# First pair's keys in three pieces, and a rewritten order of every engine's work, in a fused attention and feed-forward kernel

## The chip, the cores and the metric

The kernel runs on 1 core of one Trainium2 chip. The metric is device time in microseconds (us) of one launch; lower is better. The engines are called as in the profile: PE (TensorE products), PEld (its weight loads), DVE (VectorE), ACT (ScalarE), POOL (GpSimd) and SP (SyncE, which only issues transfers here).

Runs are compared in one state, "fast": not more than 1.5% above the fastest of the same kernel; the others are called slow. A **look** is the one run of a kernel that was profiled. Every ratio below is the mean time of one kernel's fast runs over the mean of the other's in the same rounds on the same chip, so it is not quite the ratio of the medians beside it. Beside each run stands the mean granted clock of PE as a share of full speed. As the records of the clock hold only 1.0 and 0.5, I work out a run's **halved time** as 2 x (1 - mean clock) x span. It is good to about 0.7 us, and I call a run with less than 2.5 us of it a run with a **whole clock**.

## The reference, cut to what matters

```python
def _attn_ref(q, k, v, proj):            # q, k, v: 4 x 8 heads x 768 x 64
    q_bits = (np.einsum('bhsd,dk->bhsk', q, proj) > 0)     # 6 sign bits per row
    k_bits = (np.einsum('bhsd,dk->bhsk', k, proj) > 0)
    # ... a bucket number from the bits, mask = equal buckets
    scores = np.where(mask, scale * np.matmul(q, k.transpose(0, 1, 3, 2)), -1000000000.0)
    # ... softmax, times v
def _moe_ref(x, w_in, w_out, alpha):     # x: 3072 x 512
    h = x @ w_in
    s = np.sin(alpha * h)
    g = h + s * s / (alpha + 1e-09)
    return (g @ w_out).astype(np.float32)
```

## The kernel before: the parts that matter

Heads are worked in pairs, counted from 0 (the expectations below say "second pair" for pair 1, "fifth pair" for pair 4). The 6 sign bits become 12 rows that are appended to the 64 rows of q and k, so that one product of 76 rows gives a masked score. For pair 0 VectorE writes those rows straight to their place. For every other pair it writes them to a tile `bits`, and four transfers, `row1` for pair 1, carry them over partitions to the tile `QK`:

```python
if pid == 0:
    def directf(o, e, t, h, c):          # eight bit strips of 12x384 for pair 0
        r = 32 * (2 * t + h)
        nc.vector.tensor_scalar(out=hold.slots["QK"][D:KR, t, h, HS * c:HS * c + HS], in0=two(hs, "nd")[c][r:r + NROW, 0:HS],
                                scalar1=cc[r:r + NROW, 0:1], scalar2=cc[r:r + NROW, 1:2], op0=ALU.is_gt, op1=ALU.mult)
# ... cut; for the other pairs:
    rows.append(dma(None, None, 50000, deps=[bt, hold], ..., name=f"row{pid}", get=get, dur=0.8, ...))
```

Every engine runs one written list of operations, in which the names mean: `ld30` the load of pair 3's queries, `ld31` of its keys, `tr` transposes, `ev` and `cast` copies, `hash` the products for the bits, `sc2.3` the scores and `ex2.3` the exponential of unit 2 (pair 1's first unit) block 3, `v` values, `win`/`wout` a weight's load, `fold`/`fo` its scaling, `alpha` a column of factors and `abc` its broadcast. An engine stands at an operation whose data are not there. The lists' starts, before:

```
SP    ld00 ld01 ld10 ld11 ld40 ld21 alpha ld20 ld31 ld30 row1 row1 row1 row1 row2 ...
POOL  cast1 cast1 v0 cast1 win2 win0 v3 wout0 cast1 win2 abc win1 v1 cast2 win0 wout2 ...
```

Where PE has nothing ready, the build puts warming products on the identity matrix into its list. Five buffers hold loaded tokens.

The softmax here doesn't subtract the row's maximum and nothing guards it: scores larger than these inputs give would overflow.

## Time and profile before

| | before |
|---|---|
| median of 3 runs, one of them slow | 334.84 us (334.49 to 341.64) |
| span of the profiled run, clock | 333.6 us, 0.995 |
| first score, first exponential | 14.16, 14.70 us |
| thirteenth exponential (pair 1's first) | 31.67 us |
| ScalarE changes from exp to sin | 72.14 us |
| from there to the end | 261.46 us |

### The profile page before, as it was taken

To read this page: it belongs to the slowest core of one execution; us is meant where nothing else is said; L and a number is where in the kernel's file an instruction comes from. 1 tells how busy PE (TensorE), PEld (TensorE's weight loads), DVE (VectorE), ACT (ScalarE), POOL (GpSimd) and SP (SyncE) were. 2 spreads that over 40 slices of the span, in tenths; PEclk is the share of its full clock that TensorE was granted. 3 is DMA by queue.
4 is the path that set the end of the run, shared out by engine and by line. 5 is a ranking of instruction groups with operands and counts; after the bars stand their busy time and mean duration, and the time that the engine had idled before them with its cause. 6 is when DMAs were issued, how large, how long until landed. Compare 5 with 4: busy or idle time off the path is not lost.

```text
span 333.6 us, 5767 instructions
## 1 busy us (share of the span) xinstructions
PE 322.3 (97%) x2088; PEld 157.9 (47%) x2088; DVE 221.3 (66%) x312; ACT 269.4 (81%) x387; POOL 156.0 (47%) x151
## 2 busy tenths in 40 slices
PE   8959999999999999999999999999999999999995
PEld 6533333355534444455554444455544444565542
DVE  2736853769887577987896867868837354295620
ACT  1747999999999988889989998988889898784401
POOL 1855498949766606328713664350643630012110
PEclk9989999999999999999999999999999999999999
DMA  8999797599927728344646033130201010100021
GB/s 216 195 323 347 112 174 222 83 192 204 171 36 102 158 46 119 51 85 72 115 71 142 10 52 64 36 93 2 32 6 64 1 67 0 67 29 2 24 96 68
DMA packets 92828, 32.95 MB, mean 99 GB/s; under 512 B 80112, under 2 KB 87552, under 8 KB 92672
## 3 DMA queue, kind: packets, MB, share of 16 engines
q1 hardware_dynamic: 85552, 20.00, 29.5%
q0 software_dynamic: 6800, 12.59, 15.5%
q8 instruction: 16, 0.26, 0.4%
q14 instruction: 12, 0.10, 0.1%
q10 hardware_dynamic: 448, 0.00, 0.1%
HBM read 28.32 MB, written 6.29 MB: 104 GB/s over the span
## 4 chain that ended last, share of the span: by engine, by line
PE 84%; ACT 6%; DMA 3%; DVE 3%; issue 2%; SPq 0%; POOL 0%; DVEq 0%; POOLq 0%; ACTq 0%
PE pb L796 24%; PE pp L647 20%; PE pp L748 18%; PE pp L689 10%; DMA tok<-in_q_dram 3%; PE pb L748 2%; ACT E L651 2%; PE pb L877 2%; PE pb L689 2%; PE pb L511 2%; PE pp L692 1%; DVE g L773 1%; PE pp L462 1%; PE pp L695 1%; PE pb L692 1%
## 5 line engine op out<-in xcount | busy, mean ns | idle before, releaser
L651 ACT ACTIVATE E<-pp 128x768 bf16<-128x768 f32 x192 | 148.3, 812 | 18.8 <-PE pp L647 17.4
L796 PE MATMUL pb<-wout,g 128*128 128x512 bf16 x384 | 100.9, 379 | 0.0
L647 PE MATMUL pp<-QK 76*128 76x384 bf16 x384 | 92.3, 328 | 0.8 <-DVE QK L538 0.3
L748 PE MATMUL pp<-xt,win 128*128 128x384 bf16 x432 | 74.8, 326 | 0.2
L662 POOL TENSOR_TENSOR sum<-E 128x768 bf16<-128x768 bf16 x27 | 40.3, 1494 | 62.7 <-ACT E L651 54.3
L748 PEld LDWEIGHTS <-win 128*128 128x128 bf16 x512 | 49.8, 98 | 37.3 <-issue 3.9
L569 POOL CAST QK<-F 64x768 bf16<-64x768 f32 x57 | 51.3, 905 | 26.4 <-DVE F L500 13.2
L773 DVE TENSOR_TENSOR g<-s,pp 128x768 bf16<-128x768 bf16 x54 | 50.7, 952 | 11.4 <-ACT s L764 5.7
L647 PEld LDWEIGHTS <-QK 76*128 76x128 bf16 x384 | 31.4, 97 | 54.1 <-issue 29.4
L796 PEld LDWEIGHTS <-g 128*128 128x128 bf16 x384 | 37.0, 97 | 35.1 <-issue 1.7
L755 ACT ACTIVATE s<-pp 128x768 bf16<-128x768 f32 x54 | 42.6, 804 | 13.5 <-PE pp L748 12.3
L766 POOL TENSOR_TENSOR s<-s 128x768 bf16<-128x768 bf16 x10 | 14.8, 1479 | 58.9 <-ACT s L755 33.2
L689 PE MATMUL pp<-E,V 128*64 128x385 bf16 x336 | 38.4, 333 | 0.2
L500 DVE STREAM_TRANSPOSE F<-tok 128x768 f32<-128x768 f32 x24 | 37.3, 1581 | 0.0
L717 DVE SCALAR_TENSOR_TENSOR xt<-pp,ln 128x384 bf16<-128x384 f32 x28 | 17.3, 620 | 25.9 <-ACT ln L714 25.1
L689 PEld LDWEIGHTS <-V 128*64 128x64 bf16 x384 | 20.1, 108 | 29.1 <-issue 24.1
L662 DVE TENSOR_TENSOR sum<-sum,E 128x768 bf16<-128x768 bf16 x44 | 26.5, 603 | 3.4 <-ACT E L651 1.9
L764 ACT ACTIVATE s<-s 128x768 bf16<-128x768 bf16 x33 | 27.8, 843 | 0.9
L662 DVE TENSOR_TENSOR sum<-sum 128x768 bf16<-128x768 bf16 x22 | 18.0, 818 | 11.2 <-POOL sum L662 10.0
L711 ACT ACTIVATE ln<-pp,epsb 128x384 f32<-128x384 f32 x28 | 16.3, 581 | 6.3 <-PE pp L695 4.4
L622 POOL TENSOR_TENSOR wout<-g,inva 128x1024 bf16<-128x1024 f32 x8 | 15.7, 1965 | 7.4 <-DMA g<-in_moe_w_out_dram 4.5
L662 DVE TENSOR_TENSOR sum<-E 128x768 bf16<-128x768 bf16 x17 | 11.5, 679 | 8.7 <-ACT E L651 8.0
(65 smaller groups left out, 259.3 us busy)
## 6 DMA issues: line engine op xcount, KB each, us to landing
out_dram<-osb SPq DMA_DIRECT2D x24, 256.0 KB
tok<-in_q_dram SPq DMA_DIRECT2D x48, 96.0 KB
tok<-in_k_dram SPq DMA_DIRECT2D x48, 96.0 KB
g<-in_moe_w_in_dram POOLq DMA_DIRECT2D x8, 512.0 KB, 7.5
g<-in_moe_w_out_dram POOLq DMA_DIRECT2D x8, 512.0 KB, 6.8
V<-in_v_dram POOLq DMA_DIRECT2D x16, 192.0 KB, 4.1
tok<-in_q_dram SPq DMA_DIRECT2D x4, 384.0 KB
tok<-in_k_dram SPq DMA_DIRECT2D x4, 384.0 KB
```

The source lines that it names most:

```text
L500: nc.vector.transpose(out=fh[0].slots["F"][:, ti, :].rearrange("p (j i a) -> p a j i", j=NJ, a=4), in_=hold_t.slots["tok"].rearrange("p (t ...
L569: nc.gpsimd.tensor_copy(out=d_, in_=s_)
L647: nc.tensor.matmul(out=o.slots["pair"][:, h, 0:HS], lhsT=qk[0:KR, 1, h, 128 * j:128 * j + 128], rhs=qk[0:KR, 0, h, c * HS:(c + 1) * HS], s ...
L651: ex = P.op("ACT", 0.695, lambda o, e, sc=sc, j=j: nc.scalar.activation(out=eh.slots["E"][:, j, :, 0:HS], in_=sc.slots["pair"][:, :, 0:HS] ...
L662: o = P.op(eng, {"DVE": 0.57, "POOL": 1.62}, lambda o, e: (nc.vector if e == "DVE" else nc.gpsimd).tensor_tensor(out=dst(), in0=a(), in1=b ...
L689: nc.tensor.matmul(out=nd[0][r, 0:HS + 1], lhsT=vt[:, h, jmap(b, j), :], rhs=et[:, j, h, 0:HS + 1], start=(j == 0), stop=(j == NJ - 1), ti ...
L717: xe = P.op("DVE", 0.6, lambda o, e: nc.vector.scalar_tensor_tensor(out=xt_hold[(b, c)].slots["xt"][:, p, :], in0=two(v0, "nd")[0][:, 0:HS ...
L748: nc.tensor.matmul(out=two(o, key)[i][:, 0:HS], lhsT=win[p][:, 128 * F:128 * F + 128], rhs=xt[:, p, :], start=(p == 0), stop=(p == NPT - 1))
L755: nc.scalar.activation(out=o.slots["s"], in_=hh.slots[key][:, :, 0:HS], func=AF.Sin)
L764: nc.scalar.activation(out=o.slots["s2"], in_=x, func=AF.Square)
L773: nc.vector.tensor_tensor(out=gt[:, 2 * s_:2 * s_ + 2, :], in0=s2, in1=hh.slots[key][:, :, 0:HS], op=ALU.add)
L796: nc.tensor.matmul(out=acc, lhsT=g_hold[(b, c)].slots["g"][:, F, 128 * tb:128 * tb + 128], rhs=wout[:, F, :], start=(F == 0), stop=(F == N ...
```

## The change

The intent: let the first scores begin before all keys have landed, and write the order of all lists anew, so that the long ScalarE wait near 21 us goes. The core of the diff:

```diff
+    def prep_first():
+        for m in range(3):               # three pieces of 128 columns of each head's keys
+            ldk.append(dma(..., 128 * S * 4 // 3, ..., name=f"ld0{m + 1}", get=get))
+        # ... per piece: transpose, copy (ev01), hash, ONE bit operation of 12x512, two small casts
+            hk = P.op("PE", 0.5, hkf, deps=[hq, ev] + ([bk[0]] if m == 2 else []), ..., name="hash0")
+            bk.append(P.op("DVE", 0.85, ..., name="bits0"))
-            for i, (t, h, c) in enumerate(((0, 0, 0), (0, 1, 0), (1, 0, 0), ...)):   # eight strips, whole q and k
-                rows.append(P.op("DVE", 0.69, ...directf..., name=f"bits{pid}"))
 # ... cut; the written lists, starts only:
-SP    ld00 ld01 ld10 ld11 ld40 ld21 alpha ld20 ld31 ld30 row1 row1 row1 row1 row2
+SP    ld00 ld11 ld10 ld01 ld03 ld21 ld02 ld30 ld20 ld40 ld31 row1 row1 row1 row1 row2 ... alpha
-POOL  cast1 cast1 v0 cast1 win2 win0 v3 wout0 cast1 win2 abc win1 v1 cast2 win0 wout2
+POOL  v0 abc cast1 cast0 cast0 cast0 cast1 cast1 wout3 v3 v1 win1 v2 win0 wout2 cast2 cast2
-ACT   proj tab proj cc cc ev10 cast0 ...
+ACT   proj proj cc cc ev00 ev00 ev01 cast0 ev10 cast0 ev11 ex0.3 ev01 ex0.0 ...
```

## The prediction

> **What bounds the kernel now.** I read the page first, then the chain of waits in order of time, then the timeline of the first 30 us engine by engine, then stretches side by side, last the DMA queues in two short windows.
>
> ```profile
> PE 322.3 (97%) x2088; PEld 157.9 (47%) x2088; DVE 221.3 (66%) x312; ACT 269.4 (81%) x387; POOL 156.0 (47%) x151
> ```
>
> TensorE (PE) looks full, but its busy time counts waiting filler products and stretched ends. So I look for stages. In the stretches table (us, then busy us and instructions of PE, weight loads, VectorE (DVE), ScalarE (ACT), GpSimd (POOL); then clock, DMA share, GB/s) the limit changes:
>
> ```profile
> 14.70:20.70 6.00, 4.36 (x40) 2.38 (x38) 4.60 (x8) 5.34 (x7) 5.83 (x13) 1.00 1.06 330
> 20.70:26.90 6.20, 3.70 (x26) 1.73 (x27) 1.65 (x3) 0.03 (x1) 1.83 (x4) 0.72 1.06 331
> 26.90:72.10 45.20, 44.62 (x332) 15.50 (x331) 26.52 (x28) 42.98 (x64) 34.45 (x29) 1.00 0.84 179
> 72.10:302.00 229.90, 229.36 (x1464) 115.75 (x1463) 170.33 (x233) 206.93 (x299) 103.75 (x90) 1.00 0.36 71
> ```
>
> From 26.9 to 72.1 us ScalarE, which takes the exponentials of batch 0 and of one unit of batch 1, is 95% busy (42.98 of 45.20): it bounds. After its table change at 72.1 PE bounds: taking 1/2.4 ns per column, its starts lie only 0.4 to 1.6 us apart in excess per 10 us up to 300 us. Before 26.9 neither bounds: from 20.7 to 26.9 ScalarE did 0.03 us of work, and the clock fell to 0.72. The timeline of the two engines tells why:
>
> ```profile
> 14.16 0.82 PE L647 MATMUL pp<-QK 76*128 76x384 bf16 x4 [0.28 <-DVE QK L538]
> ...
> 23.20 1.05 PE L462 MATMUL pp<-ident,tok 128*128 128x128 f32 x4 [4.09 <-DMA tok<-in_q_dram]
> ...
> 14.70 0.81 ACT L651 ACTIVATE E<-pp 128x768 bf16<-128x768 f32 x1 [0.41 <-PE pp L647]
> ...
> 26.87 1.51 ACT L651 ACTIVATE E<-pp 128x768 bf16<-128x768 f32 x2 [6.21 <-PE pp L647]
> ...
> 72.14 1.28 ACT L392 ACT_TABLE_LOAD   x1
> ```
>
> The first scores start at 14.16, the first exponential at 14.70; seven are done by 20.66; then PE, which takes its instructions in written order, stands before the transposes of pair 3's queries until their load is complete, and ScalarE stands 6.21 us behind it. The chain names the same load, issued at 12.68:
>
> ```profile
> 12.68 10.39 DMA tok<-in_q_dram
> 23.20 1.48 PE pp L462 x6
> ```
>
> Why 10.39 us for 384 KB? The queues from 18 to 23 us:
>
> ```profile
> DMA packets 667, 1.49 MB, mean 299 GB/s; under 512 B 64, under 2 KB 370, under 8 KB 667
> q0 software_dynamic: 597, 1.41, 99.3%
> q1 hardware_dynamic: 70, 0.09, 4.8%
> ```
>
> Weights (4096-byte packets, issued by GpSimd) moved 1.41 MB, the token queue (1536-byte packets, issued by SyncE) 0.09 MB. Of the 16 landings of that load 13 came by 19.4 us; the last at 23.07.
>
> **What the Trainium skill says.** "DMA: Bandwidth & Descriptors", section "Queues, rings and completion order": each DMA engine goes round-robin between queues a packet at a time, a packet holding several descriptors. The trace agrees that the queues interleave, but the split is far from even: 16 to 1 in bytes here. "Latency and other measured facts" on the same page: engines 7 and 15 are usually slower, perhaps from software descriptor rings; three of sixteen landings coming late fits that, though I did not resolve which engines. "ScalarE: Activation LUTs", section "What ACT_TABLE_LOAD costs": about 1283 ns; the trace has 1.28 us.
>
> **The change part by part.** (1) First pair. Before: all of q and k land, are transposed (6 products, 0.70 us), copied, hashed together; VectorE then makes eight bit strips of 12x384 at 0.674 us, four of which precede the first score. After: q alone first; keys in three pieces of 128 columns per head, each with its transpose, copy, hash, one bit operation of 12x512, and two small casts. A 12x512 operation I put at 0.674 + 128/0.96 ns = 0.81 us, so all bits cost 4 x 0.674 + 3 x 0.81 = 5.1 us against 5.4: hardly less work. What matters is when the first is ready.
>
> I follow the new written order with durations of the trace. PE again runs 22 fillers first, so the first transpose starts near 6.2 (6.24 in the chain) and ends at 6.95. Two ScalarE copies of 0.43 each: 7.85. Hash: 8.4. First key piece transposed by 8.75; the loads now stand q0, k1, q1, then the first piece: 1.31 MB, and in the trace 1.18 MB had landed at 6.9 and 1.57 MB at 8.5, so it is there. VectorE: a cast 0.6 from 7.9, three query strips 3 x 0.67, a small cast 0.35, the key strip 0.8: 11.7. So the first score starts near 11.8 instead of 14.16.
>
> ScalarE gives most of that back. Before the first exponential the order puts two q halves (to 7.85), a piece's copy (0.4, from 8.75), a small cast (0.4), two halves of a pair-1 tensor (0.86, from 10.2), a cast 0.83, two more halves 0.86: 12.7. Then comes a table load: the operation that loaded it at 1.36 us before now stands late in ScalarE's order, so the load (1.28) is made directly before the first exponential. 12.7 + 1.28 = 14.0, against 14.70. Gain: 0.7 us.
>
> (2) The order of loads. The broadcast alpha (1 MB, 8 KB rows) is now issued second on GpSimd, at about 8 us by my count (the projection has landed at 5.9, its copies on VectorE and GpSimd end at 7.0, issuing V takes 0.9), so its bytes move from some 11.5 to 14.5; the other weights follow only after six casts, at about 18, their bytes near 20. Pair 2 and 3's keys and queries are ahead of the 128-byte transposed load of pair 4, and the 2048-packet alpha column comes later. By the trace's 0.29 MB per us for these loads, pair 3's queries land about 12, pair 2's about 16.5, pair 3's keys about 21. PE's order reaches them after 6, 8 and 11 scores, i.e. when ScalarE has freed the score buffers: about 17.8, 20 and 22. None should hold it. The 6.2 us wait goes. Pair 3's keys have only 1 us in hand before the weights take the bandwidth again; I allow 1 us of new wait.
>
> (3) ScalarE takes over copies after its first exponential: a key piece (0.4) and a whole tensor of pair 3 that VectorE copied before (0.86): +1.3 us.
>
> Sum at ScalarE's first change to sin: -0.7 - 6.2 + 1.3 + 1.0 = -4.6 us, so at 67.5 instead of 72.1. GpSimd must keep up: cut finer, the same table has it busy 9.87, 8.61 and 10.72 us in 40 to 50, 50 to 60 and 60 to 72, which is 29.2 of 32. The new order takes three of the eight folds of w_out (1.9 us each) off it and gives it one more of w_in (2.4): about 3.3 us less, which pays for most of the earlier date.
>
> (4) From 72 us on work and counts are the same (64 sin, 192 score groups, 192 contractions, the same table changes). PE is the bound, so the lead passes through to the end; the order is rewritten there too, which I take as 0, give or take 1.5 us.
>
> 334.8 - 4.6 = 330.2, rounded to 330.3: 1.3% less.
>
> **The rivals.** (a) The wait returns under another name: pair 3's keys or pair 2's queries are caught by the alpha or w_out bytes, as pair 3's queries were. For: the 16 to 1 split, the late three of sixteen landings. Against: the order leaves 14.5 to 20 us free of weights. It would give back 2 to 5 us: 332 to 335. (b) GpSimd binds: folds of w_in are late, the first expansion waits; its 40 to 72 us stretch speaks for it, the three moved folds against. 332 to 334. (c) The new order is also better later: 14 us of small gaps after 72 us are there to be had, and the load model behind the order is now nearer to the trace. With the full 6.2 + 0.7 us and 1 to 2 us of that, 327. (d) The pieces are what pays, the first exponential at 12 us: then the start gains 2 to 3 us more, 328; the written place of the table load speaks against it.
>
> **Range and chances.** Main case 330.3; (a) and (b) pull to 333.5, (c) and (d) to 327. Eight in ten: 327.0 to 333.3. Faster by over 2% means under 328.1, which needs 6.7 us: 0.22. Within 2%: 0.76. Slower: 0.02, as the start would have to wait longer than now.
>
> **What would show it.** Right: first score near 11.8, a table load just ahead of the first exponential at about 14.0; no PE wait over 1.5 us for a token load between 14 and 30; twelve exponentials by 26 us; the change to sin near 67.5; the same distance from there to the end (262 us) within 1.5 us. Wrong: a token load of over 8 us from issue to landing that PE waits for (a); a wait of the first expansion on a w_in fold (b); a first exponential before 13 (d); a distance from the change to sin to the end that is over 2 us shorter (c).

## More of the kernel before

The kernel has two stages. Up to the change to sin ScalarE, with its exponentials, is the bound, so an idle microsecond of ScalarE there is a lost microsecond. After it PE is the bound. The prediction shows the lines that say so.

## The result, and the profile after

| | before | after |
|---|---|---|
| median of the rounds | 337.87 (334.49 to 341.64, 4 runs, 2 of them slow) | 332.14 (331.76 to 332.70, 4 runs) |
| ratio of fast runs, 95% interval | | 0.9926 (0.9900 to 0.9952) |
| profiled span, clock | 333.6, 0.995 | 330.4, 0.999 |
| first score, first exponential | 14.16, 14.70 | 12.11, 13.88 |
| thirteenth exponential | 31.67 | 27.80 |
| change to sin | 72.14 | 69.23 |
| from there to the end | 261.46 | 261.17 |

Against the 334.84 that the prediction starts from the median fell by 2.7 us; the ratio makes 2.5, the two profiled spans 3.2. The forecast was 4.5. Stretches of the kernel before from the first exponential to the change to sin, cut at the thirteenth; the columns are start and end, length, then busy us and instructions of PE, PEld, DVE, ACT and POOL, then clock, DMA share and GB/s:

```profile
14.70:31.67 16.97, 12.82 (x110) 5.93 (x110) 8.58 (x15) 9.78 (x13) 9.86 (x18) 0.90 1.06 341
31.67:72.14 40.47, 39.90 (x288) 13.67 (x288) 24.20 (x24) 38.60 (x59) 32.25 (x26) 1.00 0.81 157
```

The same view of the kernel after:

```profile
13.88:26.56 12.68, 11.66 (x112) 6.31 (x111) 7.31 (x14) 10.94 (x16) 9.47 (x15) 1.00 0.98 221
26.56:31.00 4.44, 3.58 (x39) 1.40 (x39) 2.29 (x4) 2.32 (x5) 2.10 (x4) 1.00 1.12 316
31.00:69.23 38.23, 37.04 (x268) 12.69 (x267) 24.66 (x26) 36.00 (x55) 26.70 (x23) 1.00 0.98 198
69.23:330.40 261.17, 254.98 (x1577) 129.34 (x1598) 180.91 (x246) 216.70 (x309) 111.23 (x98) 1.00 0.33 68
```

Read ScalarE's column. Before, it is busy 9.78 + 38.60 = 48.38 of 57.44 us and idle 9.06. After, it is busy 10.94 + 2.32 + 36.00 = 49.26 of 55.35 and idle 6.09. So the exponentials' stage gains 0.82 at its start, loses 0.88 to added copies and gains 2.97 of idle time; 0.29 more comes after it: 3.2 in sum. The wait of 6.21 that the prediction shows is gone, but only 2.97 of it is gained; 3.2 us of other waits have come. The timeline of ScalarE after shows the four that I count as new:

```profile
12.58 1.28 ACT L394 ACT_TABLE_LOAD   x1
13.88 0.81 ACT L735 ACTIVATE E<-pp 128x768 bf16<-128x768 f32 x1
15.46 0.37 ACT L503 COPY F<-pb 128x256 f32<-128x256 f32 x1 [0.77 <-PE pb L499]
...
23.47 1.69 ACT L735 ACTIVATE E<-pp 128x768 bf16<-128x768 f32 x2 [0.37 <-PE pp L731]
...
27.80 0.81 ACT L735 ACTIVATE E<-pp 128x768 bf16<-128x768 f32 x1 [1.24 <-PE pp L731]
29.46 0.81 ACT L735 ACTIVATE E<-pp 128x768 bf16<-128x768 f32 x1 [0.86 <-PE pp L731]
...
69.23 1.28 ACT L394 ACT_TABLE_LOAD   x1
```

The brackets hold the idle time before an instruction and what ended it. 0.77 is a wait for the third key piece's transposes (L499), 1.24 and 0.86 are waits for scores (L731). These four make 3.24. What is left of the idle time is 2.85 us in both looks (9.06 - 6.21 and 6.09 - 3.24), in waits of at most 0.6 us each, not all at the same places; I treat it as unchanged. Ahead of the scores behind 0.37 and 0.86 PE's list puts hash and value products. PE's timeline names what the thirteenth score itself waited for:

```profile
12.11 0.82 PE L731 MATMUL pp<-QK 76*128 76x384 bf16 x4
...
27.42 0.34 PE L731 MATMUL pp<-QK 76*128 76x384 bf16 x1 [1.25 <-DMA QK<-bits]
```

`QK<-bits` are the rows of pair 1. The first was issued at 18.35, the fourth at 20.87, and that one's last part landed at 27.38: 6.5 us for 18 KB. Pair 3's keys, the token load that SyncE issued just ahead of the rows, had landed at 20.88, so the fourth row did not wait behind them. The queues from 20 to 27 us:

```profile
q0 software_dynamic: 977, 1.55, 100.6%
q1 hardware_dynamic: 200, 0.21, 8.8%
```

The columns are packets, MB and the share of the 16 engines' time. q0 holds what GpSimd issues (weights and values), q1 what SyncE issues (here the rows and the last of the token loads).

### The profile page after: what moved, and what is told of

Read it like the earlier page. It is cut to its first block, busy times and chain, and to the rows that moved or that the text cites. A ratio compares the mean times of both kernels' runs of the same rounds, so it can differ in the third digit from the quotient of the medians.

```text
span 330.4 us, 5749 instructions
## 1 busy us (share of the span) xinstructions
PE 319.3 (97%) x2078; PEld 158.2 (48%) x2101; DVE 220.2 (67%) x311; ACT 272.6 (82%) x394; POOL 153.4 (46%) x152
## 4 chain that ended last, share of the span: by engine, by line
PE 75%; ACT 7%; DVE 4%; issue 2%; SPq 1%; DMA 1%; DVEq 0%; ACTq 0%
PE pb L880 24%; PE pp L832 19%; PE pp L731 16%; PE pp L773 8%; ACT E L735 4%; PE pb L832 3%; PE pb L611 2%; PE pb L773 1%; PE pp L779 1%; DVE g L857 1%; DVE QK L661 1%; DMA tok<-in_k_dram 1%; ACT s L839 1%; PE pp L611 1%; PE pb L776 1%
## 5 line engine op out<-in xcount | busy, mean ns | idle before, releaser
L880 PE MATMUL pb<-wout,g 128*128 128x512 bf16 x361 | 98.2, 379 | 1.0 <-issue 0.2
L731 PE MATMUL pp<-QK 76*128 76x384 bf16 x384 | 92.0, 327 | 2.5 <-DMA QK<-bits 1.2
L746 POOL TENSOR_TENSOR sum<-E 128x768 bf16<-128x768 bf16 x29 | 42.5, 1473 | 53.6 <-ACT E L735 50.4
L731 PEld LDWEIGHTS <-QK 76*128 76x128 bf16 x384 | 31.6, 97 | 53.5 <-issue 25.4
L773 PE MATMUL pp<-E,V 128*64 128x385 bf16 x324 | 36.3, 333 | 0.4 <-DVE g L857 0.4
L746 DVE TENSOR_TENSOR sum<-sum,E 128x768 bf16<-128x768 bf16 x44 | 28.6, 650 | 4.4 <-ACT E L735 2.8
L801 DVE SCALAR_TENSOR_TENSOR xt<-pp,ln 128x384 bf16<-128x384 f32 x27 | 16.5, 610 | 13.9 <-ACT ln L798 13.4
L746 DVE TENSOR_TENSOR sum<-sum 128x768 bf16<-128x768 bf16 x22 | 15.4, 698 | 15.2 <-POOL sum L746 14.8
L891 DVE COPY osb<-pb 128x512 f32<-128x512 f32 x16 | 11.0, 690 | 13.9 <-PE pb L880 13.9
L798 ACT ACTIVATE ln<-ln 128x384 f32<-128x384 f32 x32 | 16.8, 525 | 0.3
```

The lines of the kernel that those rows point to most:

```text
L731: nc.tensor.matmul(out=o.slots["pair"][:, h, 0:HS], lhsT=qk[0:KR, 1, h, 128 * j:128 * j + 128], rhs=qk[0:KR, 0, h, c * HS:(c + 1) * HS], s ...
L746: o = P.op(eng, {"DVE": 0.57, "POOL": 1.62}, lambda o, e: (nc.vector if e == "DVE" else nc.gpsimd).tensor_tensor(out=dst(), in0=a(), in1=b ...
L773: nc.tensor.matmul(out=nd[0][r, 0:HS + 1], lhsT=vt[:, h, jmap(b, j), :], rhs=et[:, j, h, 0:HS + 1], start=(j == 0), stop=(j == NJ - 1), ti ...
L798: rc = P.op("ACT", 0.42, lambda o, e: nc.scalar.activation(out=ln.slots["ln"], in_=ln.slots["ln"], func=AF.Exp, scale=-1.0), deps=[ln], pr ...
L880: nc.tensor.matmul(out=acc, lhsT=g_hold[(b, c)].slots["g"][:, F, 128 * tb:128 * tb + 128], rhs=wout[:, F, :], start=(F == 0), stop=(F == N ...
```

## The experiments

18 runs of kernels were made in five calls, each call on one chip beside the kernel before; two are the changed kernel itself. All gave correct results. The first theory, T: the long wait's gain is eaten by the new short waits, and each can be had back by itself. Its main rival, R: pair 1's rows land when they land, so whatever is saved ahead of the thirteenth exponential comes back as a longer wait for them. The variants of the changed kernel have its number of warming products written down as a table; line numbers shift by 5.

### What sets the thirteenth exponential

**weights_early** and **weights_late**: four weight loads moved on POOL.

```diff
-POOL  v0 abc cast1 cast0 cast0 cast0 cast1 cast1 wout3 v3 v1 win1 v2 win0 wout2 cast2 cast2   (changed)
+POOL  v0 abc wout3 win1 win0 wout2 cast1 cast0 cast0 cast0 cast1 cast1 v3 v1 v2 cast2 cast2   (weights_early)
+POOL  v0 abc cast1 cast0 cast0 cast0 cast1 cast1 v3 v1 v2 cast2 cast2 wout3 win1 win0 wout2   (weights_late)
```

> The changed kernel, fillers kept number for number, with one edit: two w_out and two w_in loads are issued right behind the alpha broadcast (about 8.5 us) and not behind the six casts (18.2 us). Theory (the order of weights against tokens carries the gain): queries of pair 2 and keys of pair 3 are caught, PE waits 3 to 6 us for token loads, and the time is back to 1.000 to 1.010 of before. Rival (the order of weights does not matter, PE or ScalarE work does): within 0.3% of the changed kernel, 0.990 to 0.996.

Measured: ratio 1.002 (0.998 to 1.006), fast runs 336.8 to 338.3. The view of PE's waits shows token loads caught behind the early weights (the look is a slow run, but both waits end by 29.70, before its clock was first halved at 30.35):

```profile
PE pp L567 <- DMA tok<-in_k_dram: 3.3, 1, 3.3
...
PE pb L567 <- DMA tok<-in_q_dram: 1.5, 1, 1.5
```

So the later place of the weights is a needed part of the change: with this one part undone its whole gain is gone.

> The changed kernel, fillers kept, with one edit: the same four weight loads are issued behind the two casts of pair 2 (about 24 us) and not at 18 to 22 us. Theory (the 2 us that my sum missed are the rows of pair 1's bits, caught by the weights): the rows land by 23 us, the waits of 1.23 and 0.86 us before the 13th and 14th exponential go, ScalarE's change to sin comes at 67 to 68 us, 0.985 to 0.989 of before. Rival (the time returns elsewhere: folds of w_in late on GpSimd): 0.990 to 0.996.

Measured: ratio 0.987 (0.982 to 0.992); four runs with a whole clock lie at 332.5 to 333.0, two slow ones at 340.3 and 342.2. The fourth row landed 4.5 us after its issue, not 6.5, and the two waits of 1.24 and 0.86 became one of 0.61. But a wait of 1.24 appeared at 49.2, and the four runs are no lower than the changed kernel's 332.1. That was on another chip, so whether the edit gains anything stays open.

**q4_late**: the query load of pair 4 behind the rows.

```diff
-SP    ... ld20 ld40 ld31 row1 row1 row1 row1 row2
+SP    ... ld20 ld31 row1 row1 row1 row1 ld40 row2      (and its transpose on VectorE two places later)
```

> The changed kernel, fillers kept, with one edit: pair 4's query load (3072 packets of 128 bytes) stands behind the rows of pair 1's bits, and its stream transpose two places later on VectorE. Theory (the rows stand behind these packets and behind pair 3's keys in one queue): rows land by 22 to 23 us and the two waits shrink by 1 to 2 us, 0.985 to 0.990 of before. Rival (pair 4's load is then caught by the weights, and its transpose holds VectorE near 33 us): 0.993 to 1.000.

Measured: ratio 1.001 (0.996 to 1.007). Pair 1's rows landed no sooner (27.86), and a later row now waited as well:

```profile
PE pp L736 <- DMA QK<-bits: 2.9, 2, 1.5
```

The rows are not held by that token load.

**changed_again** and **changed_third**: the changed kernel itself, as yardsticks.

> The changed kernel itself, instruction for instruction (its clock-warming products written down as a table instead of chosen by the scheduler). It is the yardstick of this call: the other three are to be compared with it on the same chip. Expected: 331.5 to 333 us in runs at a clock of 0.995 or more, a ratio to the kernel before between 0.985 and 0.995. If its runs are as scattered here as those of the variants of the first call (332.5 to 342), the scatter is a matter of this kernel's stage and not of the variants' edits.

Measured, changed_again: ratio 0.9938 (0.9873 to 1.0004), runs 331.6 to 335.8 and a slow one, 341.6. So the scatter belongs to the changed kernel too.

**table_early**: the exponential's table at the start, and the first two exponentials ahead of the copy of the third piece.

```diff
-ACT   proj proj cc cc ev00 ev00 ev01 cast0 ev10 cast0 ev11 ex0.3 ev01 ex0.0 ...
+ACT   proj tab proj cc cc ev00 ev00 ev01 cast0 ev10 cast0 ev11 ex0.3 ex0.0 ev01 ...
```

> The changed kernel with the exponential's table loaded second on ScalarE instead of just ahead of the first exponential, and the first exponential ahead of the third piece's copy, so that it can follow the first scores (which end near 13.1) directly. Theory A (what is lost at the start is lost at the end): first exponential at 12.6 to 13.3 instead of 13.9, change to sin 0.6 to 1.2 us sooner, time lower by as much. Theory B (the first pair's twelve exponentials have slack behind them, because the second pair's rows land at about 27.4 whatever was done before): the start gains the same 0.6 to 1.2, the wait of ScalarE ahead of its thirteenth exponential grows from 1.2 to 1.8 to 2.4, and the time stays within 0.3 us.

Measured: ratio 0.998 (0.991 to 1.005). ScalarE's timeline:

```profile
13.28 1.51 ACT L740 ACTIVATE E<-pp 128x768 bf16<-128x768 f32 x2 [1.26 <-PE pp L736]
15.77 0.37 ACT L508 COPY F<-pb 128x256 f32<-128x256 f32 x1 [0.97 <-PE pb L504]
...
28.78 0.81 ACT L740 ACTIVATE E<-pp 128x768 bf16<-128x768 f32 x1 [1.90 <-PE pp L736]
```

The first exponential is 0.42 us sooner than in changed_again (13.70), the thirteenth 0.91 later. The start's gain was given back, as R says, and more, because the rows landed at 28.36.

**table_early_weights_late**: both edits.

> Both edits: the exponential's table early with the first exponential ahead of the third piece's copy, and the four weight loads issued behind the casts of the second pair, near 24 us, instead of ahead of them. If theory B is right, the early start is worth something only with the second pair's rows early too: the change to sin then comes 1.2 to 2 us sooner than in the changed kernel, the time is 330 to 331 on a chip where the changed kernel takes 332. Theory A alone expects no more than what the early table gives by itself. Rival: the weights landing later make the later stage wait (a token load of pairs 4 or 5 behind them), and the gain of the start is given back between 49 and 64 us.

Measured: ratio 0.997 (0.988 to 1.005); runs 333.2 to 347.7. The expected 330 to 331 was missed. In this look the rows were issued only from 20.95, against 18.77 in changed_again, and landed at 28.02. The thirteenth exponential came at 29.70, 1.68 us later and right behind the twelfth, so the rows did not hold it. Token loads of pair 3 had held PE (0.73 us for queries, 1.27 for keys), and ScalarE was idle 0.80 and 1.35 us behind them: waits that this combination brings, earlier than the rival's 49 to 64 us.

**third_piece_early**: the third piece's transposes ahead of the hash that waits for VectorE.

```diff
-PE    ... sc0.0 sc0.3 tr01 hash0 tr01 sc1.3 ...
+PE    ... sc0.0 sc0.3 tr01 tr01 hash0 sc1.3 ...
```

> The changed kernel with the transposes of the third key piece two places earlier on TensorE, ahead of the second piece's hash product that waits for VectorE's bits, so that ScalarE's copy of that piece can start at about 14.7 (end of the first exponential) instead of 15.1 to 15.5. Theory A: ScalarE's 0.77 us wait behind its first exponential falls to 0 to 0.3, the change to sin comes 0.4 to 0.7 us sooner and the time is lower by that. Theory B (the second pair's rows land at 27.4 whatever went before): the wait goes, the one ahead of the thirteenth exponential grows by as much, the change to sin stays where it was within 0.3 us when the clock isn't halved.

Measured: ratio 0.984 (0.978 to 0.990), five of six runs at 331.0 to 332.4. The look was better than expected, with the change to sin at 67.93.

> The changed kernel again, instruction for instruction, as the yardstick on the chip of this call. Expected: 331.5 to 334 us in runs whose clock is never halved; the three others are compared with it directly.

> The version with the third piece's transposes two places earlier, now on the same chip as the changed kernel. The look of the call before gave 5.2 us of idle time of ScalarE between the first exponential and the change to sin instead of 6.1, and the change to sin at 67.9 instead of 69.2. If that is the edit's doing: runs with a whole clock 0.5 to 1.3 us below the changed kernel's. Rival: the difference was the start's scatter (the first transpose began at 5.43 instead of 5.82, because the clock was granted full at 4.8 instead of 5.6), and the two kernels agree within 0.4 us.

Measured: both ratios 0.9898 (0.984 to 0.996 and 0.987 to 0.993). With a whole clock the changed kernel took 332.0 to 333.6 (4 runs), this one 331.0 to 333.4 (12 runs): medians 332.30 and 332.27. Nothing. The timeline says why:

```profile
14.05 0.81 ACT L740 ACTIVATE E<-pp 128x768 bf16<-128x768 f32 x1
14.76 0.37 ACT L508 COPY F<-pb 128x256 f32<-128x256 f32 x1
...
16.06 0.81 ACT L740 ACTIVATE E<-pp 128x768 bf16<-128x768 f32 x1 [0.22 <-PE pp L736]
17.50 0.81 ACT L740 ACTIVATE E<-pp 128x768 bf16<-128x768 f32 x1 [0.63 <-PE pp L736]
...
27.89 0.81 ACT L740 ACTIVATE E<-pp 128x768 bf16<-128x768 f32 x1 [0.91 <-PE pp L736]
```

The wait of 0.77 is gone; 0.22 and 0.63 stand in its place, and the thirteenth exponential is where it was. In this look PE's timeline blames another engine for the thirteenth score:

```profile
27.29 0.32 PE L736 MATMUL pp<-QK 76*128 76x384 bf16 x1 [1.12 <-POOL QK L662]
```

That is a trap: where an instruction waits for several semaphores, the page names one. The third row landed at 27.15, when that cast ended too, and the first of the score's two products began 0.14 us after it, as in the changed kernel (25.72 and 25.85). There the same cast ran until 26.73, so the product does not need it. The second product needs the fourth row. Its landing settles the rest. For each look with the changed order of loads, the landing of the last of pair 1's rows and the start of the thirteenth exponential:

| look | last row landed | thirteenth exponential | between | from it to sin |
|---|---|---|---|---|
| changed kernel | 27.38 | 27.80 | 0.42 | 41.43 |
| changed_again | 27.45 | 27.87 | 0.42 | 42.57 (clock halved 3.4 us in it) |
| changed_third | 27.11 | 27.52 | 0.41 | 41.45 |
| table_early | 28.36 | 28.78 | 0.42 | 44.05 (halved 6.8 us) |
| q4_late | 27.86 | 28.28 | 0.42 | 45.58 (halved 6.8 us) |
| fewer_warmers | 27.40 | 27.82 | 0.42 | 50.02 (halved 17.1 us) |
| third_piece_early | 26.52 | 26.94 | 0.42 | 40.99 |
| third_piece_early_again | 27.47 | 27.89 | 0.42 | 41.43 |
| third_early_fewer_warmers | 26.69 | 27.11 | 0.42 | 41.44 |
| weights_late | 25.99 | 27.09 | 1.10 | 41.99 |
| third_early_weights_late | 25.81 | 26.63 | 0.82 | 40.75 |
| table_early_weights_late | 28.02 | 29.70 | 1.68 | 41.02 |
| weights_early | 30.37 | 32.82 | 2.45 | 48.23 (halved 11.2 us) |

Nine times the exponential follows the landing by 0.41 or 0.42 us, whatever was done ahead of it. R holds: the rows bind, and T's picture of waits that can be had back one by one falls. The four looks in which the weights' place was changed are the exception. With late weights the last row landed 4.3 to 4.5 us after its issue, with early weights (the rows were then issued behind them, at 24.2 to 26.8) 3.6, against 5.6 to 7.2 in the other nine, and the rows no longer bind. So the weights' bytes hold up the rows, by about 2 us of the 6.5; what makes the other 4 us was not tested.

**third_early_weights_late**: both.

> As third_piece_early, with the four weight loads behind the second pair's casts as well. Theory B: now the rows come early enough, so the 0.77 us and the 1.2 and 0.9 us of the rows' waits all go in part: from the first exponential to the change to sin 53.5 to 54.5 us instead of 55.35, if the clock stays whole. With a whole clock its runs are at or below 332, lower than the changed kernel's by 0.7 to 1.5. Rival: the later weights move the wait to 47 to 48 us as they did before (1.24 us), and the sum stays at 54.6.

Measured: ratio 0.986 (0.979 to 0.992); six runs with a whole clock, 330.4 to 334.3, median 332.25, beside 331.98 for the five fast runs of third_piece_early. The profile has what was expected:

```profile
25.93 1.52 ACT L740 ACTIVATE E<-pp 128x768 bf16<-128x768 f32 x2
28.05 1.51 ACT L740 ACTIVATE E<-pp 128x768 bf16<-128x768 f32 x2 [0.61 <-PE pp L736]
```

Twelfth and thirteenth run back to back, and from the first exponential to sin it took 53.22 us, not 55.35. The first exponential, however, came at 14.16, later than in the changed kernel. The timed runs don't show the gain, so I don't claim it.

**fewer_warmers** and **third_early_fewer_warmers**: 12 warming products at the start instead of 22, alone and with the third piece early.

```diff
-FILL = {20: 22, 23: 9, 51: 7, 38: 7, 154: 2, 56: 2}      # warming products ahead of a PE operation
+FILL = {20: 12, 23: 9, 51: 7, 38: 7, 154: 2, 56: 2}
```

> The changed kernel with 12 clock-warming products ahead of the first transpose instead of 22, which end near 3.9 us instead of 6.0. If TensorE's warmers hold up the first transposes (query tokens landed at 3.96, first transpose at 5.8), the first score comes up to 1.5 us sooner. Rivals: the projection matrix, landing at 5.7, holds the hash, so the gain is at most 0.5; or the clock is granted full later than 5.6 and every transpose of the start takes longer, so that the first score is no earlier or later. In both cases the time is within 0.5 us of the changed kernel's.

Measured: ratio 0.992 (0.985 to 0.999), four runs with a whole clock at 331.4 to 333.4. The first transpose began at 3.90, not 5.64 as in changed_again.

> The third piece's transposes early and 12 warming products instead of 22 at the start. In the earlier look with 12 the first transpose began at 3.9 instead of 5.8 though the clock was granted full only at 6.7, and the first scores ended 0.4 to 0.5 sooner. Expected: first score 0.3 to 0.8 sooner than in the version without this edit, and with a whole clock a time lower by 0 to 0.8 us. Rival: the rows of the second pair catch the exponentials all the same, and the gain of the start is in the wait ahead of the thirteenth.

Measured: ratio 0.986 (0.982 to 0.991). Five runs with a whole clock at 331.14 to 331.52 (median 331.44), beside the changed kernel's 331.97 to 333.57 (median 332.30) on the same chip: 0.9 us less, the best version, and one slow run at 343.8. Here the rows were issued from 18.21 and landed at 26.69, against 18.56 and 27.11 in changed_third. So an earlier start is worth something where it brings the rows' issue forward; the two looks show 0.43 us of it at the change to sin (68.55 and 68.97), and the rest of the 0.9 they don't explain:

```profile
13.06 0.81 ACT L740 ACTIVATE E<-pp 128x768 bf16<-128x768 f32 x1
...
27.11 0.81 ACT L740 ACTIVATE E<-pp 128x768 bf16<-128x768 f32 x1 [1.41 <-PE pp L736]
```

### Pieces or order: which part pays

**pieces_old_loads**: one part undone; the pieces and the other engines' new lists kept.

```diff
-SP    ld00 ld11 ld10 ld01 ld03 ld21 ld02 ld30 ld20 ld40 ld31 row1 ... alpha
+SP    ld00 ld11 ld10 ld01 ld03 ld21 ld02 ld40 alpha ld30 ld20 ld31 row1 ...
```

> The changed kernel with one part undone: the fifth pair's query load and the weights' column of factors are back at their old places, ahead of the fourth pair's query load and of the second pair's rows. It keeps the pieces. Theory (the order of the loads carries the gain): ScalarE's long wait returns near 20 to 27 us with 3 to 6 us, TensorE stands still in it and its clock is halved for at least one window of 3.4 us; time equal to the kernel before's within 1 us, ratio 0.995 to 1.005. Rival (the pieces carry it): the ratio stays at 0.99 or below.

Measured: ratio 0.9957 (0.9925 to 0.9990), median 335.5 of 18 fast runs of 22. PE's and ScalarE's timelines, the same wait as before:

```profile
22.04 1.22 PE L567 MATMUL pb<-ident,tok 128*128 128x128 f32 x6 [3.39 <-DMA tok<-in_q_dram]
```

```profile
23.94 0.81 ACT L740 ACTIVATE E<-pp 128x768 bf16<-128x768 f32 x1 [4.16 <-PE pp L736]
```

The first exponential stays early (13.74), the thirteenth goes back to 31.53, sin to 72.75. So without the new place of these two loads nearly all that the profile shows is lost (3.5 us at the change to sin), and the pieces with the rest of the new lists give almost nothing there; the ratio leaves them about 1.4 us, which the two looks (334.0 us, and 333.6 before) don't show. As weights_early lost the whole gain by another part alone, the parts' shares do not add up: each is needed.

The reverse, the order without the pieces, I tried five times, and each try broke on a new wait of its own. All start from the kernel before.

```diff
-SP    ld00 ld01 ld10 ld11 ld40 ld21 alpha ld20 ld31 ld30 row1 row1 row1 row1 row2
+SP    ld00 ld01 ld10 ld11 ld21 ld20 ld31 ld30 row1 row1 row1 row1 ld40 alpha row2         (old_loads_late)
+      the same, with win2 win1 win0 wout2 behind cast2 on POOL                           (old_pieces_new_loads)
+SP    ld00 ld01 ld10 ld11 ld21 alpha ld20 ld31 ld30 row1 row1 row1 row1 ld40 row2         (old_pieces_q_late, weights late too)
+SP    ld00 ld01 ld10 ld11 ld21 alpha ld30 ld20 ld40 ld31 row1 row1 row1 row1 row2         (old_pieces_token_order)
+      the same, with win2 win1 win0 wout2 behind cast2 on POOL                           (old_pieces_token_order_wl)
```

> The kernel before, with one edit: the 128-byte load of pair 4's queries and the alpha column are issued behind the four rows of pair 1's bits. No pieces, old written order elsewhere. Theory (the order of the loads is what paid): pair 3's queries are then complete before the weights start at 17 us, the wait of 6.2 us falls under 2 us, the first exponential stays at 14.7, and the time is 0.987 to 0.992 of before. Rival (the pieces are what paid): the wait only changes its name (rows, pair 4) and the time is 0.996 to 1.004.

> The kernel before with the other part alone: the fifth pair's query load and the column of factors behind the second pair's rows, as in the first call, and the four weight loads issued next by GpSimd behind the second pair's casts, so that the rows do not share the bandwidth with them and TensorE does not stand still near 26 us. Theory (the first call's 51 us of halved clock came from that pause): the clock stays whole or is halved for a window or two, no wait of ScalarE above 1 us up to 40 us, ratio 0.985 to 0.995, which is then the load order's part by itself. Rival (the clock is halved for another reason than that pause, such as TensorE's lower load without the pieces): clock 0.92 to 0.97 again and a ratio of 1.02 to 1.04.

> The kernel before with only the fifth pair's query load behind the second pair's rows, and four weight loads behind the second pair's casts. The column of factors stays at its old place: in the two earlier tries it had been moved too, and VectorE then stood 8 to 10 us at the operation that needs it, which held up the values' evictions and with them TensorE. Theory (that was what broke those tries): no wait of ScalarE above 1.5 us before 50 us, a clock that stays whole or is halved for one or two windows, a ratio of 0.983 to 0.993, which is then the order's part without the pieces: 2.5 to 5.5 us. Rival 1 (without the pieces the stage is too thin for the clock gate): clock 0.92 to 0.97 and a ratio above 1.02 again. Rival 2 (pieces and order are worth something only together): no halved clock, a ratio of 0.995 or more.

> The kernel before with the token loads in the order that the change gives them: the fifth pair's query load from fifth to ninth place, behind the third and fourth pairs' query loads, but still ahead of the fourth pair's key load and of the second pair's rows. Everything else as before: whole keys for the first pair, the weights and the column of factors where they were. The earlier tries put that query load behind the rows, where VectorE and the third pair's rows then waited for it for 6 us: those tries were broken by the edit, this one repeats what the change does. Theory (the order carries the gain and needs no pieces): ScalarE's 6.2 us wait falls to 1 to 3 us, the change to sin comes 2 to 4 us sooner, ratio 0.985 to 0.995. Rival 1 (order and pieces pay only together): a wait of 4 us or more stays and the ratio is 0.995 to 1.005. Rival 2: another stop of TensorE above 2 us near 36 us halves the clock for 17 us or more, ratio above 1.02.

> As old_pieces_token_order, with four of GpSimd's weight loads behind the second pair's casts, so that the second pair's rows do not share the bandwidth with them. Theory: 0.5 to 1.5 us less waiting for the rows than in old_pieces_token_order and as much less time. Rival: the weights then come late to VectorE and GpSimd, which scale them in the order of their queues, and a new wait near 35 to 48 us costs as much or more, with the clock halved if TensorE stands still for 2 us.

| run | ratio | runs, us | the wait that its look shows |
|---|---|---|---|
| old_loads_late | 1.037 (1.030 to 1.043) | 346.7 to 354.7 | VectorE 8.3 us for the column of factors |
| old_pieces_new_loads | none, mostly slow runs | 345.2 to 358.3 | the same, 10.0 us |
| old_pieces_q_late | 1.038 (1.030 to 1.047) | 346.1 to 355.8 | VectorE 6.2 us for pair 4's queries, PE 6.1 for rows |
| old_pieces_token_order | 0.998 (0.992 to 1.004) | 331.8 to 365.4 | PE 7.8 us for pair 3's keys |
| old_pieces_token_order_wl | none, mostly slow runs | 330.7 to 364.0 | PE 7.2 us for pair 3's keys |

The lines behind the table, one fence for each of the first four; columns are the total, the number of waits and the longest:

```profile
DVE inva L596 <- DMA alpha<-in_moe_alpha_dram: 8.3, 1, 8.3
```

```profile
DVE inva L600 <- DMA alpha<-in_moe_alpha_dram: 10.0, 1, 10.0
```

```profile
PE pp L652 <- DMA QK<-bits: 6.5, 2, 6.1
...
DVE F L505 <- DMA tok<-in_q_dram: 6.2, 1, 6.2
```

```profile
PE pp L467 <- DMA tok<-in_k_dram: 7.8, 1, 7.8
```

The expectation of the first call, 0.987 to 0.992, was missed by far, and so was that of all the others. All five looks are slow runs. The first three put a load behind the rows that another engine's list needs sooner; that was my edit's fault. In old_loads_late, however, the clock was halved at 27.79, before VectorE's wait began (28.74) and after PE had waited 1.1 us for rows, so that wait did not start the halving; in the other four the waits begin before it. The last two repeat the order that the change gives the token loads, and there PE's old list reaches the transposes of pair 3's keys too early. The best single runs, 331.8 and 330.7, beside 332.4 for the best run of the kernel before, hint at what the order could give; what it gives without the pieces and without the other engines' new lists stays open. What these tries show is that a new order in one list did not pay while the lists of the other engines were not written for it.

### The clock

In the looks above a second cost appears. The stretches of fewer_warmers and, below it, of old_loads_late, whose looks are both slow runs:

```profile
31.00:57.40 26.40, 24.79 (x176) 7.84 (x175) 18.15 (x19) 25.21 (x39) 15.20 (x17) 1.00 0.91 198
57.90:75.00 17.10, 16.37 (x72) 4.54 (x71) 7.25 (x6) 8.86 (x13) 11.50 (x7) 0.50 0.82 147
```

```profile
27.80:79.00 51.20, 51.20 (x211) 11.48 (x210) 21.63 (x21) 30.62 (x42) 28.28 (x23) 0.50 0.69 129
```

At a clock of 0.50 PE is busy throughout, and ScalarE falls from 95% busy (25.21 of 26.40) to 52% (8.86 of 17.10): the bound has moved to PE. fewer_warmers has 14.3 us of idle ScalarE in its stage, the changed kernel 6.1; 8.2 of the 14.3 lie in the 17.1 us at half clock. The halving began at 57.94, inside this gap of PE:

```profile
58.63 0.53 PE L778 MATMUL pb<-E,V 128*64 128x385 bf16 x2 [2.09 <-DVE xt L806]
```

The Trainium skill, "TensorE: Matmul & The Clock Gate", section "What's actually happening", has a free-running window of 3413 ns and only two states. The records agree: in 20 looks only 1.0 and 0.5 occur, and the halved stretches inside a run are 3.4, 6.8, 10.2, 17.1, 41.0, 44.4, 51.2 and 64.9 us long, all whole multiples of 3.413. Its section "HAM oscillation — how this bites in real kernels" warns of PE gaps above about 3.4 us. Here shorter ones went with a halving: it came 1.40 us into the gap of 2.09 in fewer_warmers, and 1.61 us after one of 1.26 in changed_again. The same 1.25 in the changed kernel's own look halved nothing. The traces say what differs. Cut each look, from its first clock record to its last full step, into steps of 3.413 us and sum PE's idle time in each step: all 11 full-clock steps with 1.48 us or more of it were followed by a halved one, none with 1.31 or less was, and of the five between (1.35 to 1.44) two were. The changed kernel's step has 1.25 us; changed_again's has 1.48, the same gap and 0.22 us of short ones beside it. So it is the sum within a step that separates them here.

The scatter of the runs goes with the clock. Before's runs of five chips, 96, have a whole clock 12 times; the changed kernel's 16 have one 12 times. With a whole clock the medians are 334.4 (332.4 to 335.8) and 332.3 (331.6 to 335.8), 2.1 us apart (not all from the same chips); over all runs, slow ones too, they are 337.8 and 333.0. That suggests that part of what the change gives in daily use is a long PE wait less, and with it a steadier clock. Each microsecond of halved time goes with 0.5 us in the runs of before (a straight line through the 96). This is a correlation; no run holds all else equal.

## Why the prediction was wrong

The direction, the class and the range were right (332.1 lies in 327.0 to 333.3), but 4.5 us of gain were forecast and 2.5 to 3.2 came. (334.84 - 4.6 makes 330.2; the 330.3 was rounded wrongly, which changes nothing.) By its own steps:

1. **The start**, "-0.7": right. First score 12.11 (forecast 11.8), table load just ahead of the first exponential at 13.88 (14.0), gain 0.82. A 12x512 bit operation took 0.811 us (0.81).
2. **The order of loads**, "The 6.2 us wait goes ... I allow 1 us of new wait": the wait went, and no token load holds PE for over 1.5 us. **The allowance is the term that failed**: 1.0 us was forecast, 3.2 was measured (0.77 + 0.37 + 1.24 + 0.86). I looked for new waits only among token loads ("Pair 3's keys have only 1 us in hand"). Pair 1's rows, which are issued at 18.35 to 20.87, just as the weights begin to move near 20, are in no line of the sum. That they must land before the thirteenth exponential is the step that is missing. They landed at 27.38 and set the thirteenth exponential at 27.80. The forecast had twelve exponentials done by 26; they were done at 26.56, and the rows added 1.24, the hash products that PE puts ahead of the next scores 0.86. The table of looks shows the rows as the bound and the weights as what delays them. The other 1.14 us, 0.77 for the third key piece and 0.37 behind a hash, have nothing to do with loads and were not forecast either.
3. **Added copies**, "+1.3": 0.88 measured. Mis-sized, in the good direction.
4. **The rest from the change to sin on**, "which I take as 0, give or take 1.5 us": right, 0.29 less.

The sum, -0.7 - 6.2 + 1.3 + 1.0 = -4.6, becomes -0.82 - 6.21 + 0.88 + 3.24 = -2.91 with the measured terms: 69.23 instead of 72.14.

The rivals. (a), a wait that returns under another name because weights catch a transfer, is what happened, with rows in place of tokens, at the low end of the 2 to 5 us that I gave it (1.24 + 0.86). Its dismissal, "the order leaves 14.5 to 20 us free of weights", overlooked that the rows are issued at the end of that stretch and still under way after it. (b), GpSimd as the bound, did not come: 26.70 of 38.23 us busy. (c), a better later order: 0.29, nearly nothing. (d), pieces that pay: the first exponential came no sooner than 13.88, and an earlier one by itself gained nothing in table_early. Not foreseen at all was the clock: the forecast compares with a kernel before whose runs carry a halved clock of varying length.

## What to carry to other kernels

When a long wait is removed, list every transfer that must land in the stretch that becomes short, the small ones too: the next bound here was an 18 KB transfer issued beside 512 KB weights. Test a suspected bound by the distance between a landing and its first user over many looks; a constant distance (0.41 or 0.42 us in nine looks) says more than the engine that one wait line names. And in a stage that is bound by another engine watch PE's clock: PE gaps of 1 to 2 us can end in a clock at half that costs more than the gaps, and short gaps close to each other add up.

## What the Trainium skill lacked or had wrong

- "TensorE: Matmul & The Clock Gate": the halved state is said to end after about 3.4 us of sustained work. In old_loads_late it lasted 51.2 us, 15 windows, with PE busy 51.20 of 51.20 as the profile models it. The section "Seeing it yourself" warns that the records can be unreliable and knows a clock stuck, at a quarter, for over 50 us; here the slow-down is real, since the mean duration of a score product was 515 ns against 330 ns in the changed kernel. What releases the clock is not settled by these runs.
- The same page: a gap above about 3.4 us is given as what throttles, and for the shorter idles that it also tells of no length is given. Here 1.48 us of idle PE, summed within a window of 3.413 us, went with a halving every time (11 of 11), and 1.31 or less never.
- The same page: that warming products can cost time at the start. With 22 of them the first transpose of the changed kernel and its variants began at 5.43 to 6.03 us, mostly the later the later the full clock was granted (4.8 to 6.9); with 12 it began at 3.90 and 3.97.
- "DMA: Bandwidth & Descriptors": what a small transfer pays beside large ones. The fourth 18 KB row transfer took 5.6 to 7.2 us from issue to landing beside the weights (nine looks), 4.3 to 4.5 with the weights late (three looks) and 3.6 behind early weights (one).
- No page that I used says it of the profile: one wait line named GpSimd's cast where the landing of the rows was the bound (third_piece_early_again: the third row landed at 27.15, the product began 0.14 us later; the fourth at 27.47, the exponential 0.42 us later).
